# A decode kernel's list scheduler is given the fetch time of TensorE instructions, finer durations, and a new order of loads

## Chip, cores, metric

The kernel runs on one core of one Trainium2 chip. The metric is the device time of one execution, in microseconds (us), median over several runs. The profile's span (first to last instruction) is about 2 us shorter than the time of the same execution. Every comparison below is between runs of state "fast"; nothing slow was seen. One core means one die, so there is no second die to compare with.

Names used below: PE is TensorE and PEld its weight loads, DVE is VectorE, ACT is ScalarE, POOL is GpSimd, and SPq is the queue that sends out the loads. A load *lands* when all of its bytes are in place. An instruction page, or *page* for short, is a block of 256 instructions that PE fetches at once (the page *of a kernel* is the profiler's summary of it). "Planner" is the list scheduler.

## The reference, cut to what matters

A decode step of four transformer layers for batch B = 4 and one new token: attention layer, feed-forward layer, and the same two again. Both attention layers read the *same* caches.

```python
B, Sq, D = 4, 1, 512
Hq, Hkv, Sk, Dh = 32, 8, 8192, 128        # k_cache, v_cache: (B, Hkv, Sk, Dh) bf16, 67 MB each

def _A_ref(x, k_cache, v_cache, wq, wo):
    q = (x @ wq) ...                       # 4 query heads share one K/V head
    p = _softmax(einsum("bhqd,bhkd->bhqk", q, k) * Dh ** -0.5)
    return einsum("bhqk,bhkd->bhqd", p, v) ... @ wo
def _B_ref(x, w_gate, w_up, w_down):       # F = 1792
    return (_silu(x @ w_gate) * (x @ w_up)) @ w_down

x = x + _A_ref(_layernorm(x), k_cache, v_cache, wq, wo)
x = x + _B_ref(_layernorm(x), w_gate, w_up, w_down)
x = x + _A_ref(_layernorm(x), k_cache, v_cache, wq, wo)
x = x + _B_ref(_layernorm(x), w_gate, w_up, w_down)
```

The second attention layer of a batch element needs the first attention and feed-forward of *that element only*. So the kernel treats the four elements as four batches and interleaves layers: while batch 0 is between its layers, batch 1 is in its first.

## The kernel before

The kernel is a program that plans itself. While it is built, it makes a list of steps with an engine, an estimated duration and dependences; a list scheduler runs them through a small model and fixes the order of instructions of every engine. The order of *loads* is not decided by the scheduler: it is a string written by hand (or by a search). The loads go out in that order, each as soon as one of ten slots of 1 MB is free.

```python
class Plan:
    HOP = 0.2                    # us between a step and a dependent step on another engine
    LOAD_LEAD = 0.8
    LOAD_TAIL = 1.4
    ...
            at, s = best                         # the step that can start first
            s.start, s.end = at, at + s.us       # its duration is a constant
            free_at[s.eng] = s.end
    ...
    def emit(self):
        for s in sorted(self.steps + self.loads, key=lambda s: (s.start, s.prio[0])):
            s.fn()

ORDER = ("KKKqKVKKKoKKKgKKKKVKVVKKKgKuKKVoKVVVKKKVKKKVVKVVKVKKVVoVoVuddVKKKVKKKVKKVKKVKKKKKVKKKVKKVKVVKKVK"
         ... )                   # K, V: one 1 MB unit of a cache; q: wq; other letters: the next weight piece
KEPT = [5, 5, 5, 5]              # per batch: V units kept in their slot from layer 0 to layer 1, not loaded twice
NSLOT = 10
VCUT = [5, 5, 5, 8]
```

A K unit (4096 positions of one head) is transposed by DVE in place (2 instructions) and multiplied by PE (32 matmuls, so 64 instructions with their weight loads). After 16 K units of a batch, the softmax of that batch runs. A V unit is 32 matmuls on PE. After all V units of a first-layer batch comes its "chain": output projection, feed-forward, layer norm, q projection. The second-layer K units of that batch can be transposed before, but not multiplied; until the chain is done, they hold their slots.

```python
        NTAIL = [0, 3, 3, 3]
        vgroups = [(0, 0, g) for g in v_first(0)]
        rest = v_first(1)
        vgroups += [(0, 1, g) for g in rest[:G - NTAIL[1]]]
        for b in range(B):
            vgroups += [(1, b, g) for g in v_second(b)[:VCUT[b]]]
            if b + 1 < B:
                vgroups += [(0, b + 1, g) for g in v_first(b + 1)[G - NTAIL[b + 1]:]]
            vgroups += [(1, b, g) for g in v_second(b)[VCUT[b]:]]
            if b + 2 < B:
                vgroups += [(0, b + 2, g) for g in v_first(b + 2)[:G - NTAIL[b + 2]]]
```

This says which V unit each V of the string is: VCUT second-layer groups of batch b go ahead of the last NTAIL first-layer groups of batch b+1.

Of the kernel before, what the change touches and what calls it, by code (L numbers as in the profile page):

```python
# [5 lines left out]
ALU = mybir.AluOpType  # L6
# [5 lines left out]
class _Rec:  # L12
    __slots__ = ("w", "r")
# [89 lines left out]
class Step:  # L103
    __slots__ = ("eng", "us", "deps", "fn", "prio", "take", "free", "start", "end", "loads", "slot_of")

    def __init__(self, eng, us, fn, deps, prio, take=None, free=None):
        self.eng, self.us, self.fn, self.prio = eng, us, fn, prio
        self.deps = [d for d in deps if d is not None]
        self.take, self.free = take, free
        self.start = self.end = None  # L110
        self.slot_of = None


class Plan:

    HOP = 0.2
# [10 lines left out]
    def add(self, eng, us, fn, deps, prio, take=None, free=None):  # L127
        s = Step(eng, us, fn, deps, prio, take, free)
        self.steps.append(s)
        return s  # L130
# [7 lines left out]
    def run(self):  # L138
# [48 lines left out]

        self.slot = {}
        left = len(self.steps)
        pump(0.0)  # L190
        while left:
            best = None
            for e in engines:
                cand = None
                for t, s in todo[e]:
                    if s.take is not None:
                        b = min(bank_free.values()) if bank_free else None
                        if b is None:
                            continue
                        t = max(t, b)  # L200
                    at = max(t, free_at[e])
                    k = (at > free_at[e] + 1e-9, at if at > free_at[e] + 1e-9 else 0.0, s.prio[0])
                    if cand is None or k < cand[0]:
                        cand = (k, at, s)
                if cand is not None and (best is None or cand[1] < best[0]):
                    best = (cand[1], cand[2])
            nxt = None
            if li < len(self.loads) and (slots or self.loads[li].slot_of is None):
                nxt = max(sp_at, min(slots)[0] if self.loads[li].slot_of is not None else 0.0)
            if best is None and nxt is None:  # L210
                raise RuntimeError("the plan is stuck")
            if best is None or (nxt is not None and nxt <= best[0]):
                pump(nxt)
                continue
            at, s = best
            s.start, s.end = at, at + s.us
            free_at[s.eng] = s.end
            for i, (_, x) in enumerate(todo[s.eng]):
                if x is s:
                    todo[s.eng].pop(i)  # L220
                    break
            if s.take is not None:
                b = min(bank_free, key=lambda x: bank_free[x])
                del bank_free[b]
                held[s.take] = b
                self.bank[s.take] = b
            if s.free is not None:
                bank_free[held.pop(s.free)] = s.end + self.HOP
            if s.slot_of is not None:
                slots.append((s.end + self.HOP, self.slot[s.slot_of]))  # L230
            left -= 1
            finish(s)
# [4 lines left out]
    def emit(self):  # L237
        for s in sorted(self.steps + self.loads, key=lambda s: (s.start, s.prio[0])):
# [3 lines left out]
ORDER = ("KKKqKVKKKoKKKgKKKKVKVVKKKgKuKKVoKVVVKKKVKKKVVKVVKVKKVVoVoVuddVKKKVKKKVKKVKKVKKKKKVKKKVKKVKVVKKVK"  # L242
         "KKKKVKKKVVKVVVVVVVKVVVVVKVKVKKKKVKKVKKKVKKVKKVKKVKVKKVVKKVVKKKKKKKKVKVVVVVVVVVVVVKKKVKKKVVKKKKKK"
         "KKVKKVVVVVVVVVVVVVVVVVKVVVKKVKKKKKKKKKKKKKVVVVVVVVVVVVV")
KEPT = [5, 5, 5, 5]
NSLOT = 10
VCUT = [5, 5, 5, 8]


def bass_interleave_layers__gqa_block_cached__swiglu_ffn__decode_kernel(  # L250
# [33 lines left out]
    with ExitStack() as es:  # L284
# [107 lines left out]
        def col_sum(src, dst, key_in, key_out, deps, tag):  # L392
            def mm():
                bk = pbk(tag)
                op("pe", lambda e: e.matmul(ps[:, bk * BW:bk * BW + NQ * B], lhsT=onesm[:],  # L395
                                            rhs=src[:].rearrange("p n b -> p (n b)"), start=True, stop=True),
                   reads=["onesm", key_in], writes=[f"pb{bk}"])

            def rd():
                bk = pbk(tag)  # L400
                op("dve", lambda e: e.tensor_reduce(dst[:], ps[:, bk * BW:bk * BW + NQ * B].rearrange("p (n b) -> p b n", b=B),  # L401
                                                    AX.X, ALU.add), reads=[f"pb{bk}"], writes=[key_out])
            a = PL.add("pe", 0.6, mm, deps, CHAIN, take=tag)
            return PL.add("dve", 0.2, rd, [a], CHAIN, free=tag)
# [19 lines left out]
        def q_scale(dep):  # L424
            return PL.add("dve", 0.2, lambda: op("dve", lambda e: e.tensor_scalar(qscale[:], rstd[:], scale, None, op0=ALU.mult),
                                                 reads=["rstd"], writes=["qscale"]), [dep], CHAIN)

        def q_proj(heads, deps, tag):
            def mm():
                bk = pbk(tag)  # L430
                for h in heads:
                    for kt in range(KT):
                        op("pe", lambda e: e.matmul(ps[:, bk * BW + h * B:bk * BW + (h + 1) * B],  # L433
                                                    lhsT=wq_sb[:, kt, h * Dh:(h + 1) * Dh],
                                                    rhs=xnT[:, kt * B:(kt + 1) * B],
                                                    start=(kt == 0), stop=(kt == KT - 1)),
                           reads=["wq", "xnT"], writes=[f"pb{bk}"], sig=(kt == KT - 1 and h == heads[-1]))
            return PL.add("pe", 0.03 * KT * len(heads), mm, deps, CHAIN, take=tag)

        def q_spread(src, n, key, deps, tag):  # L440
# [9 lines left out]
            return PL.add("pe", 0.6, mm, deps, CHAIN, take=tag)  # L450
# [11 lines left out]
        def make_qpad1(b, dep, prior):  # L462
            k = kpos[(0, b)] % 2

            def fn():
                op("dve", lambda e: e.tensor_copy(q_diag(k, 0, G), qs1[:, :, :, :, b]),
                   reads=["qs1"], writes=[f"qpad{k}_0", f"qpad{k}_1"])
            st = PL.add("dve", 0.3, fn, [dep, prior], CHAIN)
            q_ready[(0, b)] = [st, st]
# [22 lines left out]
        def q_half(b, hf, mm_tag, deps, prior):  # L492
# [9 lines left out]
            s1 = PL.add("dve", 0.25, scl, deps, CHAIN, free=mm_tag)  # L502
# [8 lines left out]
            return PL.add("dve", 0.25, cp, [sp, prior], CHAIN, free=tag)  # L511
# [24 lines left out]
        def k_pair(u, ld, prio, prev):  # L536
# [3 lines left out]
            for h in range(2):  # L540
# [4 lines left out]
                tr.append(PL.add("dve", 1.22, t, [ld], prio))  # L545
# [18 lines left out]
            st = PL.add("pe", 1.95, qk, tr + [qd, prev] + (scores_free[0] or []), prio)  # L564
# [3 lines left out]
        def softmax(l, b, lastq, prio):  # L568
# [3 lines left out]
            for a in range(4):  # L572
# [10 lines left out]
                ex.append(PL.add("act", 0.9, x, [mx] + (p_free[q] or []), CHAIN))  # L583
# [5 lines left out]
            s = PL.add("dve", 0.2, g1, [mx], CHAIN)  # L589
# [5 lines left out]
            s = PL.add("pe", 0.3, g2, [s], CHAIN, take=n + "a")  # L595
# [12 lines left out]
            s = PL.add("pe", 0.5, g4, [s], CHAIN, take=n + "b")  # L608
# [4 lines left out]
            s = PL.add("dve", 0.2, g5, [s], CHAIN, free=n + "b")  # L613
# [11 lines left out]
            s = PL.add("dve", 1.3, g7, [al], CHAIN)  # L625
            for f in range(2):
# [13 lines left out]
                t_ = PL.add("pe", 1.1, tr, [s] if f == 0 else [s, t_], CHAIN, take=f"{n}t{f}")  # L640
                e_ = PL.add("act", 1.1, ev, [t_], CHAIN, free=f"{n}t{f}")
# [14 lines left out]
            s = PL.add("pe", 0.6, w2, [s], CHAIN, take=n + "l")  # L656
# [5 lines left out]
            inv_ready[(l, b)] = PL.add("dve", 0.4, w3, [s], CHAIN, free=n + "l")  # L662
# [4 lines left out]
        def oproj(l, g, deps, prio):  # L667
# [10 lines left out]
            return PL.add("pe", 0.55, fn, deps, prio)  # L678

        def v_group(l, b, g, lds, prios):  # L680
# [3 lines left out]
            for i, cp in enumerate(VCP):  # L684
# [15 lines left out]
                st = PL.add("pe", 1.0, pv, [prev, p_ready[(l, b)], lds.get(u)], prios[i], take=tag if i == 0 else None)  # L700
# [9 lines left out]
            n = PL.add("dve", 0.2, nm, [prev, inv_ready[(l, b)]], CHAIN, free=tag)  # L710
# [5 lines left out]
        def ffn_mm(w_sb, wname, deps, tag):  # L716
# [10 lines left out]
            return PL.add("pe", 1.75, fn, deps + [w_load[f"{wname}0"], w_load[f"{wname}1"]], CHAIN, take=tag)  # L727

        def ffn(dep, tag, dst=None, dkey="x"):
# [9 lines left out]
            s = PL.add("dve", 0.25, a1, [gate, root], CHAIN, free=tag + "g")  # L739
# [3 lines left out]
            s = PL.add("act", 0.3, a2, [s], CHAIN)  # L743
# [6 lines left out]
            s = PL.add("dve", 0.9, a3, [s], CHAIN)  # L750
# [6 lines left out]
            s = PL.add("dve", 0.45, a4, [s, up], CHAIN, free=tag + "u")  # L757
# [10 lines left out]
            s = PL.add("pe", 1.75, dn, [s, w_load["wd0"], w_load["wd1"]], CHAIN, take=tag + "d")  # L768
            return add_x(XT, "x", tag + "d", [s], dst, dkey)

        def add_x(base, key, tag, deps, dst=None, dkey="x"):
# [7 lines left out]
            return PL.add("dve", 0.2, fn, deps, CHAIN, free=tag)  # L779
# [34 lines left out]
        NTAIL = [0, 3, 3, 3]  # L814
# [78 lines left out]
        sx = PL.add("pe", 0.3, start_x, [boot], CHAIN, take="x")  # L893
        sx = PL.add("dve", 0.4, start_x2, [sx], CHAIN, free="x")
        cen, root = layer_norm(sx, "i")
        late = PL.add("dve", 2.0, setup_late, [cen], [-9.0])
# [56 lines left out]
        s = PL.add("pe", 0.6, fin1, [s], CHAIN, take="out")  # L953
# [42 lines left out]
```

## Time and profile before

| | before |
|---|---|
| time, median | 673.8 us when the prediction was made, 673.35 us in the run beside the changed kernel |
| span | 670.1 us |
| bytes on the load queue | 261.38 MB in 128 K, 108 V and 11 weight loads |
| last cache load lands | 654.2 us, 15.9 us before the end |
| what landings come late, summed | 28.4 us |

The last row is worked out from the trace: for each cache load, the time from the landing before it to its own, less the median of those times (2.485 us for 1.05 MB), summed over all cache loads.

First the page of the kernel before: busy time of the engines, the 40 slices of DMA share and GB/s, the queues, and the chain that ended last.

```profile
PE 459.3 (69%) x10672; PEld 272.4 (41%) x10672; DVE 377.7 (56%) x568; ACT 48.6 (7%) x114; POOL 2.7 (0%) x8
DMA  8999999999999999999899999999799999899890
GB/s 356 415 399 420 395 419 419 419 418 393 363 416 420 415 408 420 420 420 417 326 423 419 420 398 421 419 420 418 305 422 421 420 420 418 314 402 422 352 375 3
q1 hardware_dynamic: 41600, 261.38, 95.6%
q8 instruction: 83, 1.36, 0.8%
DMA 65%; PE 20%; DVE 9%; issue 4%; SPq 1%; ACT 1%; DVEq 0%
```

No engine is near full; the load queue is. So read the GB/s row first: 419 to 420 is a full slice, and each number well below is lost time (326, 305 and 314 in slices of 16.75 us, and the last three). The windows view gives the same by stretch. Its columns are the stretch, the busy time and number of instructions of PE, PEld, DVE, ACT and POOL, the granted clock, the DMA share and GB/s.

```profile
60.00:70.00 10.00, 4.26 (x71) 1.03 (x63) 3.14 (x3) 0.00 (x0) 0.00 (x0) 0.67 1.01 419
320.00:330.00 10.00, 7.68 (x227) 5.02 (x224) 5.54 (x9) 0.00 (x0) 0.00 (x0) 0.58 0.78 293
470.00:490.00 20.00, 14.03 (x357) 8.02 (x354) 14.90 (x19) 0.50 (x2) 0.00 (x0) 0.59 0.82 322
580.00:590.00 10.00, 9.05 (x268) 5.53 (x264) 5.93 (x12) 0.00 (x0) 0.00 (x0) 0.61 0.78 289
630.00:650.00 20.00, 13.39 (x418) 12.88 (x419) 1.70 (x10) 2.05 (x2) 0.00 (x0) 0.50 0.87 353
```

Why does the queue starve at 320? The timeline there (start, duration, instruction, and in brackets how long the engine sat idle before it and what ended that):

```profile
317.92 2.99 PE L433 MATMUL ps<-xnT,wq_sb 128*128 128x4 bf16 x107
322.86 0.70 PE L433 MATMUL ps<-xnT,wq_sb 128*128 128x4 bf16 x21 [1.95 <-issue]
324.65 0.28 PE L446 MATMUL ps<-qT,ident 128*32 128x16 bf16 x16
326.89 4.19 SPq L92 DMA_DIRECT2D pool<-in_A_k_cache_dram  x4
```

The q projection of a chain stops for 1.95 us in its middle, with no semaphore to wait for. "issue" means that. Only after the q projection and spreading (L446) can the waiting K units be multiplied, their slots come free, and four loads go out in a bunch at 326.9. That the stop is an instruction fetch is read from its pattern: PE has 21344 instructions (matmuls and weight loads), queue 8 moved 83 packets of 16 KB, one for 257 instructions, and in dense stretches those packets come 6.1 to 6.3 us apart. PE's waits on "issue" sum to 28.5 us, 13 of them over 1 us. Counting PE's instructions in the trace settles it: the three stops between 460 and 476 us come 256 instructions apart, and so do the last three, at 640, 646 and 652 us.

The end of the kernel, as the chain of waits tells it (start, duration, what):

```profile
639.68 0.51 PE ps L694 x19
640.19 2.00 issue
645.74 2.66 issue
651.95 2.66 issue
658.08 0.93 PE ps L694 x32
```

After the last softmax, PE has 16 V units and 8 pieces of output projection to do, 1280 instructions, and stops at three pages. It is done 5.6 us after the last load has landed.

### The profile page before, as it was taken

The numbers are of one execution on the slowest core, as the hardware profiler recorded it, in microseconds if no ns is written. First come the engines' busy times: TensorE is split into PE (matmuls) and PEld (weight loads), VectorE is DVE, ScalarE is ACT, GpSimd is POOL, SyncE is SP. The second block draws the span as 40 slices with busy tenths as digits, with TensorE's granted clock in tenths as the row PEclk, the third lists the DMA queues.
The fourth block names the chain that finished last, engine by engine and source line by source line (L and its number), as shares of the span: only waits on it lengthen the run. The fifth ranks groups of instructions, "written<-read, shape, count | busy, mean of one in ns | idle before, by whom it ended". The sixth has DMA issues, their size and how long they took to land.

```text
span 670.1 us, 22609 instructions
## 1 busy us (share of the span) xinstructions
PE 459.3 (69%) x10672; PEld 272.4 (41%) x10672; DVE 377.7 (56%) x568; ACT 48.6 (7%) x114; POOL 2.7 (0%) x8
## 2 busy tenths in 40 slices
PE   0555586676777687767777587777767765866566
PEld 0411153336532262357422253256422564722466
DVE  6467754544567867553476666742758502579302
ACT  1000110003000110021000110021000200000300
POOL 1000000000000000000000000000000000000000
PEclk9976565555555585555655585655656555577555
DMA  8999999999999999999899999999799999899890
GB/s 356 415 399 420 395 419 419 419 418 393 363 416 420 415 408 420 420 420 417 326 423 419 420 398 421 419 420 418 305 422 421 420 420 418 314 402 422 352 375 3
DMA packets 41693, 262.82 MB, mean 392 GB/s; under 512 B 3960, under 2 KB 9856, under 8 KB 10880
## 3 DMA queue, kind: packets, MB, share of 16 engines
q1 hardware_dynamic: 41600, 261.38, 95.6%
q8 instruction: 83, 1.36, 0.8%
q14 instruction: 10, 0.08, 0.0%
HBM read 261.36 MB, written 0.00 MB: 390 GB/s over the span
## 4 chain that ended last, share of the span: by engine, by line
DMA 65%; PE 20%; DVE 9%; issue 4%; SPq 1%; ACT 1%; DVEq 0%
DMA pool<-in_A_k_cache_dram 33%; DMA pool<-in_A_v_cache_dram 32%; PE ps L694 7%; PE ps L556 7%; DVE pool L544 6%; PE ps L433 2%; DVE negm L574 1%; SPq L92 1%; PE ps L632 1%; PE ps L672 1%; PE ps L721 1%; ACT pp L638 1%; PE ps L395 1%; PE ps L763 0%; DVE pp L623 0%
## 5 line engine op out<-in xcount | busy, mean ns | idle before, releaser
L544 DVE STREAM_TRANSPOSE pool<-pool 128x1024 uint32<-128x1024 uint32 x256 | 304.5, 1224 | 122.5 <-DMA pool<-in_A_k_cache_dram 117.0
L556 PE MATMUL ps<-pool,qpad 32*32 32x512 bf16 x4096 | 245.7, 571 | 77.4 <-DVE pool L544 72.1
L694 PE MATMUL ps<-pp,pool 128*128 128x4 bf16 x4096 | 125.1, 166 | 70.2 <-DMA pool<-in_A_v_cache_dram 51.3
L694 PEld LDWEIGHTS ps<-pp,pool 128*128 128x128 bf16 x4096 | 117.4, 104 | 105.9 <-DMA pool<-in_A_v_cache_dram 78.2
L556 PEld LDWEIGHTS ps<-pool,qpad 32*32 32x32 bf16 x4096 | 68.4, 113 | 207.2 <-DVE pool L544 133.7
L707 DVE TENSOR_TENSOR oT<-ps,invL 128x4 bf16<-128x4 f32 x64 | 10.3, 161 | 97.2 <-PE ps L694 97.2
L578 ACT ACTIVATE pp<-ps,negm 128x512 bf16<-128x512 f32 x32 | 21.5, 685 | 448.5 <-DVE negm L574 448.5
L433 PE MATMUL ps<-xnT,wq_sb 128*128 128x4 bf16 x640 | 18.4, 166 | 21.4 <-DMA wq_sb<-in_A_wq_dram 14.6
L672 PEld LDWEIGHTS ps<-oT,wo_sb 128*128 128x128 bf16 x640 | 20.6, 104 | 20.4 <-issue 11.9
L672 PE MATMUL ps<-oT,wo_sb 128*128 128x4 bf16 x640 | 23.3, 167 | 8.2 <-issue 2.7
L574 DVE TENSOR_REDUCE negm<-ps 128x1 f32<-128x512 f32 x32 | 19.8, 678 | 13.9 <-PE ps L556 13.9
L433 PEld LDWEIGHTS ps<-xnT,wq_sb 128*128 128x128 bf16 x640 | 18.5, 105 | 21.8 <-DMA wq_sb<-in_A_wq_dram 14.7
L638 ACT ACTIVATE pp<-ps 128x1024 bf16<-128x1024 bf16 x16 | 16.4, 1023 | 27.5 <-PE ps L632 27.4
L632 PE MATMUL ps<-ident,pp 128*128 128x128 bf16 x128 | 13.9, 278 | 5.1 <-ACT pp L638 3.3
L632 PEld LDWEIGHTS ps<-ident,pp 128*128 128x128 bf16 x128 | 10.6, 126 | 7.4 <-ACT pp L638 3.8
L419 ACT ACTIVATE lnv<-var,eps_sb 128x4 f32<-128x4 f32 x10 | 3.0, 297 | 112.5 <-DVE var L401 112.5
L763 PE MATMUL ps<-hT,wd_sb 128*128 128x4 bf16 x280 | 8.3, 166 | 3.4 <-issue 1.9
L721 PE MATMUL ps<-xnT,wu_sb 128*128 128x4 bf16 x280 | 8.2, 166 | 2.8 <-DVE oT L707 1.4
L623 DVE TENSOR_SCALAR pp<-pp,alpha 128x512 bf16<-128x512 bf16 x32 | 9.0, 343 | 1.8 <-ACT alpha L616 1.8
L763 PEld LDWEIGHTS ps<-hT,wd_sb 128*128 128x128 bf16 x280 | 7.9, 104 | 3.7 <-issue 3.0
L721 PEld LDWEIGHTS ps<-xnT,wu_sb 128*128 128x128 bf16 x280 | 7.9, 104 | 3.1 <-issue 1.6
L721 PEld LDWEIGHTS ps<-xnT,wg_sb 128*128 128x128 bf16 x280 | 8.8, 107 | 0.0
(65 smaller groups left out, 115.1 us busy)
## 6 DMA issues: line engine op xcount, KB each, us to landing
pool<-in_A_k_cache_dram SPq DMA_DIRECT2D x128, 1024.0 KB, 10.0
pool<-in_A_v_cache_dram SPq DMA_DIRECT2D x108, 1024.0 KB, 11.9
wq_sb<-in_A_wq_dram SPq DMA_DIRECT2D x1, 4096.0 KB, 18.4
wo_sb<-in_A_wo_dram SPq DMA_DIRECT2D x4, 1024.0 KB, 18.3
wg_sb<-in_B_w_gate_dram SPq DMA_DIRECT2D x2, 896.0 KB, 19.5
wu_sb<-in_B_w_up_dram SPq DMA_DIRECT2D x2, 896.0 KB, 19.7
wd_sb<-in_B_w_down_dram SPq DMA_DIRECT2D x2, 896.0 KB, 20.2
pp<-in_A_x_dram SPq DMA_DIRECT2D x1, 4.0 KB
```

The lines of the kernel that those rows point to most:

```text
L433: op("pe", lambda e: e.matmul(ps[:, bk * BW + h * B:bk * BW + (h + 1) * B], lhsT=wq_sb[:, kt, h * Dh:(h + 1) * Dh], rhs=xnT[:, kt * B:(kt ...
L544: op("dve", lambda e: e.transpose(v, v), reads=[key], writes=[key])
L556: op("pe", lambda e: e.matmul(ps[32 * c:32 * (c + 1), a * BW:(a + 1) * BW], lhsT=qpad[rows, qbuf, es_, g, :], rhs=ap[h][rows, :, es_ // 2, ...
L574: op("dve", lambda e: e.tensor_reduce(negm[:, q, a:a + 1], bank(a), AX.X, ALU.max, negate=True), reads=[f"pb{a}"], writes=[f"negm{q}_{a}"])
L578: op("act", lambda e: e.activation(pblk(q)[:, :, a, :], bank(a).rearrange("p (t j) -> p t j", j=32), ACTF.Exp, bias=negm[:, q, a:a + 1], s ...
L632: op("pe", lambda e: e.matmul(stg[:, t * P:(t + 1) * P], lhsT=pp[:, q, blk * P:(blk + 1) * P], rhs=ident[:], is_transpose=True, start=True ...
L638: op("act", lambda e: e.activation(pp[:, q, f * 1024:(f + 1) * 1024], bank_bf(bk)[:, :], ACTF.Copy), reads=[f"pb{bk}"], writes=pk(q))
L672: op("pe", lambda e: e.matmul(ps[:, OPJ * BW + nq * B:OPJ * BW + (nq + 1) * B], lhsT=wo_sb[:, h, nq * P:(nq + 1) * P], rhs=oT[:, l, h, :], ...
L694: op("pe", lambda e: e.matmul(ps[:, bk * BW:bk * BW + REP], lhsT=ap[:, t * Dh:(t + 1) * Dh], rhs=pp[:, q, col:col + REP], start=(i == 0 an ...
L707: op("dve", lambda e: e.tensor_tensor(oT[:, l, g * REP:(g + 1) * REP, b], ps[:, bk * BW:bk * BW + REP], invL[:, q, g * REP:(g + 1) * REP], ...
L721: op("pe", lambda e: e.matmul(ps[:, bk * BW + fo * B:bk * BW + (fo + 1) * B], lhsT=w_sb[:, kt, fo * P:(fo + 1) * P], rhs=xnT[:, kt * B:(kt ...
L763: op("pe", lambda e: e.matmul(ps[:, bk * BW + nq * B:bk * BW + (nq + 1) * B], lhsT=wd_sb[:, fo, nq * P:(nq + 1) * P], rhs=hT[:, fo * B:(fo ...
```

## The change

Its intent is to let the scheduler know that TensorE's instructions arrive in pages of 256, 6.2 us apart (what dense stretches showed), to correct the durations of the steps from a trace, and to search load order, kept units and group order again under that model. No instruction changes its work; the number of PE instructions is the same.

```diff
 class Plan:
-    HOP = 0.2
+    HOP = 0.06
+    PAGE = 6.2
+    PAGE_N = 256
...
+        def fetched(at, s):
+            nonlocal pe_n, page_at
+            if s.eng != "pe" or s.n == 0:
+                return at + s.us
+            first, pe_n = pe_n, pe_n + s.n
+            for k in range(first // self.PAGE_N + 1, pe_n // self.PAGE_N + 1):
+                there = at + s.us * (k * self.PAGE_N - first) / s.n
+                at += max(0.0, page_at + self.PAGE - there)
+                page_at = max(there, page_at + self.PAGE)
+            return at + s.us
...
-            s.start, s.end = at, at + s.us
+            s.start, s.end = at, fetched(at, s)
...
-ORDER = ("KKKqKVKKKoKKKgKKKKVKVVKKKgKuKKVoKVVVKKKVKKKVVKVVKVKKVVoVoVuddVKKKVKKKVKKVKKVKKKKKVKKKVKKVKVVKKVK"
+ORDER = ("VKdVKqKKKVKKKKKKKgKKKKVoVVKKKVKKKKVKKKVuKVVVVKVKuKKKVVVVgoodoVKVKVKKKKKKKKKKKKKKKVKKVVVVKVVVKKV"
...  (two more lines each; 13 V follow the last K before, 18 now)
-KEPT = [5, 5, 5, 5]
+KEPT = [5, 5, 4, 3]
-VCUT = [5, 5, 5, 8]
+VCUT = [1, 1, 0, 1]
+NTAIL = [0, 7, 5, 2]
...
-            st = PL.add("pe", 1.95, qk, tr + [qd, prev] + (scores_free[0] or []), prio)
+            st = PL.add("pe", 1.95, qk, tr + [qd, prev] + (scores_free[0] or []), prio, n=64)
...  (some 30 more steps get n, a duration changed by up to 1.2 us and mostly by under 0.2, or both)
-        NTAIL = [0, 3, 3, 3]
```

More of the change, by code (lines that the diff above doesn't have):

```diff
@@ L103, with __init__ @@
 class Step:
-    __slots__ = ("eng", "us", "deps", "fn", "prio", "take", "free", "start", "end", "loads", "slot_of")
-    def __init__(self, eng, us, fn, deps, prio, take=None, free=None):
+    __slots__ = ("eng", "us", "deps", "fn", "prio", "take", "free", "start", "end", "loads", "slot_of", "n")
+    def __init__(self, eng, us, fn, deps, prio, take=None, free=None, n=0):
+        self.n = n
         self.eng, self.us, self.fn, self.prio = eng, us, fn, prio
@@ L125, in __init__, with add @@
         self.bank = {}
-    def add(self, eng, us, fn, deps, prio, take=None, free=None):
-        s = Step(eng, us, fn, deps, prio, take, free)
+    def add(self, eng, us, fn, deps, prio, take=None, free=None, n=0):
+        s = Step(eng, us, fn, deps, prio, take, free, n)
         self.steps.append(s)
@@ L186, in pump @@
                 finish(s)
+        pe_n = 0
+        page_at = 0.0
+        def fetched(at, s):
[8 more added lines that the diff above has]
+            return at + s.us
         self.slot = {}
@@ L239, in emit @@
             s.fn()
-ORDER = ("KKKqKVKKKoKKKgKKKKVKVVKKKgKuKKVoKVVVKKKVKKKVVKVVKVKKVVoVoVuddVKKKVKKKVKKVKKVKKKKKVKKKVKKVKVVKKVK"
-         "KKKKVKKKVVKVVVVVVVKVVVVVKVKVKKKKVKKVKKKVKKVKKVKKVKVKKVVKKVVKKKKKKKKVKVVVVVVVVVVVVKKKVKKKVVKKKKKK"
-         "KKVKKVVVVVVVVVVVVVVVVVKVVVKKVKKKKKKKKKKKKKVVVVVVVVVVVVV")
-KEPT = [5, 5, 5, 5]
+ORDER = ("VKdVKqKKKVKKKKKKKgKKKKVoVVKKKVKKKKVKKKVuKVVVVKVKuKKKVVVVgoodoVKVKVKKKKKKKKKKKKKKKVKKVVVVKVVVKKV"
+         "KVKVKVKVKVKKKKVVKVVKKVKVKKVVKKVVVKKKKVVKKKKVVVVKKVKVKKKVKKVKVKKVKVVVKVKKVKVKKKVVKKKKKKVKKKKVKVK"
+         "VKKVVVVVVVVVVVVVVVVVVVVKVVKVKKKKKKKKKKKKKKVVVVVVVVVVVVVVVVVV")
+KEPT = [5, 5, 4, 3]
 NSLOT = 10
-VCUT = [5, 5, 5, 8]
+VCUT = [1, 1, 0, 1]
+NTAIL = [0, 7, 5, 2]
 def bass_interleave_layers__gqa_block_cached__swiglu_ffn__decode_kernel(
@@ L402, in rd @@
                                                     AX.X, ALU.add), reads=[f"pb{bk}"], writes=[key_out])
-            a = PL.add("pe", 0.6, mm, deps, CHAIN, take=tag)
-            return PL.add("dve", 0.2, rd, [a], CHAIN, free=tag)
+            a = PL.add("pe", 0.6, mm, deps, CHAIN, take=tag, n=8)
+            return PL.add("dve", 0.17, rd, [a], CHAIN, free=tag)
         def layer_norm(dep, tag):
@@ L424, in q_scale @@
         def q_scale(dep):
-            return PL.add("dve", 0.2, lambda: op("dve", lambda e: e.tensor_scalar(qscale[:], rstd[:], scale, None, op0=ALU.mult),
+            return PL.add("dve", 0.13, lambda: op("dve", lambda e: e.tensor_scalar(qscale[:], rstd[:], scale, None, op0=ALU.mult),
                                                  reads=["rstd"], writes=["qscale"]), [dep], CHAIN)
@@ L437, in mm @@
                            reads=["wq", "xnT"], writes=[f"pb{bk}"], sig=(kt == KT - 1 and h == heads[-1]))
-            return PL.add("pe", 0.03 * KT * len(heads), mm, deps, CHAIN, take=tag)
+            return PL.add("pe", 0.029 * KT * len(heads), mm, deps, CHAIN, take=tag, n=2 * KT * len(heads))
         def q_spread(src, n, key, deps, tag):
@@ L449, in mm @@
                            reads=["ident", key], writes=[f"pb{bk}"], sig=(es_ == NES - 1 and a == 3))
-            return PL.add("pe", 0.6, mm, deps, CHAIN, take=tag)
+            return PL.add("pe", 0.3, mm, deps, CHAIN, take=tag, n=32)
         def q_diag(k, g0, ng):
@@ L467, in fn @@
                    reads=["qs1"], writes=[f"qpad{k}_0", f"qpad{k}_1"])
-            st = PL.add("dve", 0.3, fn, [dep, prior], CHAIN)
+            st = PL.add("dve", 0.23, fn, [dep, prior], CHAIN)
             q_ready[(0, b)] = [st, st]
@@ L501, in scl @@
                    reads=[f"pb{bk}", "qscale"], writes=[f"qT2_{hf}"])
-            s1 = PL.add("dve", 0.25, scl, deps, CHAIN, free=mm_tag)
+            s1 = PL.add("dve", 0.21, scl, deps, CHAIN, free=mm_tag)
             tag = f"qs{b}_{hf}"
@@ L510, in cp @@
                    reads=[f"pb{bk}"], writes=[f"qpad{k}_{hf}"])
-            return PL.add("dve", 0.25, cp, [sp, prior], CHAIN, free=tag)
+            return PL.add("dve", 0.21, cp, [sp, prior], CHAIN, free=tag)
         home = {}
@@ L544, in t @@
                     op("dve", lambda e: e.transpose(v, v), reads=[key], writes=[key])
-                tr.append(PL.add("dve", 1.22, t, [ld], prio))
+                tr.append(PL.add("dve", 1.23, t, [ld], prio))
             qd = q_ready[(l, b)][2 * g // G]
@@ L582, in softmax @@
                 mx = PL.add("dve", 0.7, m, [lastq], CHAIN)
-                ex.append(PL.add("act", 0.9, x, [mx] + (p_free[q] or []), CHAIN))
+                ex.append(PL.add("act", 0.8, x, [mx] + (p_free[q] or []), CHAIN))
             scores_free[0] = ex
@@ L588, in g1 @@
                    reads=[f"negm{q}_{a}" for a in range(4)], writes=["gm"])
-            s = PL.add("dve", 0.2, g1, [mx], CHAIN)
+            s = PL.add("dve", 0.16, g1, [mx], CHAIN)
             def g2():
@@ L594, in g2 @@
                    reads=["gm", "identf"], writes=[f"pb{pbk(n + 'a')}"])
-            s = PL.add("pe", 0.3, g2, [s], CHAIN, take=n + "a")
+            s = PL.add("pe", 0.37, g2, [s], CHAIN, take=n + "a", n=2)
             def g3():
@@ L607, in g4 @@
                    reads=["rowm", "one1"], writes=[f"pb{bk}"])
-            s = PL.add("pe", 0.5, g4, [s], CHAIN, take=n + "b")
+            s = PL.add("pe", 0.58, g4, [s], CHAIN, take=n + "b", n=8)
             def g5():
@@ L612, in g5 @@
                 op("dve", lambda e: e.tensor_copy(gm[:], ps[:, bk * BW:bk * BW + 1]), reads=[f"pb{bk}"], writes=["gm"])
-            s = PL.add("dve", 0.2, g5, [s], CHAIN, free=n + "b")
+            s = PL.add("dve", 0.16, g5, [s], CHAIN, free=n + "b")
             def g6():
@@ L624, in g7 @@
                        reads=[f"pp{q}_{a}", f"alpha{q}"], writes=[f"pp{q}_{a}"])
-            s = PL.add("dve", 1.3, g7, [al], CHAIN)
+            s = PL.add("dve", 1.14, g7, [al], CHAIN)
             for f in range(2):
@@ L639, in ev @@
                        reads=[f"pb{bk}"], writes=pk(q))
-                t_ = PL.add("pe", 1.1, tr, [s] if f == 0 else [s, t_], CHAIN, take=f"{n}t{f}")
-                e_ = PL.add("act", 1.1, ev, [t_], CHAIN, free=f"{n}t{f}")
+                t_ = PL.add("pe", 1.0, tr, [s] if f == 0 else [s, t_], CHAIN, take=f"{n}t{f}", n=16)
+                e_ = PL.add("act", 1.03, ev, [t_], CHAIN, free=f"{n}t{f}")
             p_ready[(l, b)] = e_
@@ L655, in w2 @@
                    reads=["onesm", "selw"], writes=[f"pb{bk}"])
-            s = PL.add("pe", 0.6, w2, [s], CHAIN, take=n + "l")
+            s = PL.add("pe", 0.58, w2, [s], CHAIN, take=n + "l", n=8)
             def w3():
@@ L661, in w3 @@
                    reads=[f"pb{bk}"], writes=[f"invL{q}"])
-            inv_ready[(l, b)] = PL.add("dve", 0.4, w3, [s], CHAIN, free=n + "l")
+            inv_ready[(l, b)] = PL.add("dve", 0.35, w3, [s], CHAIN, free=n + "l")
         opj_n = [0]
@@ L677, in fn @@
                         opj_n[0] += 1
-            return PL.add("pe", 0.55, fn, deps, prio)
+            return PL.add("pe", 0.57, fn, deps, prio, n=32)
         def v_group(l, b, g, lds, prios):
@@ L699, in pv @@
                                reads=pk(q) + [key], writes=[f"pb{bk}"], sig=(h == 1 and t == NB - 1))
-                st = PL.add("pe", 1.0, pv, [prev, p_ready[(l, b)], lds.get(u)], prios[i], take=tag if i == 0 else None)
+                st = PL.add("pe", 1.0, pv, [prev, p_ready[(l, b)], lds.get(u)], prios[i], take=tag if i == 0 else None,
+                            n=64)
                 if not (l == 0 and (g, cp) in kept_of[b]):
@@ L709, in nm @@
                    reads=[f"pb{bk}", f"invL{q}"], writes=[f"oT{l}_{g}"])
-            n = PL.add("dve", 0.2, nm, [prev, inv_ready[(l, b)]], CHAIN, free=tag)
+            n = PL.add("dve", 0.17, nm, [prev, inv_ready[(l, b)]], CHAIN, free=tag)
             if l == 0 or b == B - 1:
@@ L726, in fn @@
                            sig=(kt == KT - 1 and fo == FO - 1))
-            return PL.add("pe", 1.75, fn, deps + [w_load[f"{wname}0"], w_load[f"{wname}1"]], CHAIN, take=tag)
+            return PL.add("pe", 1.64, fn, deps + [w_load[f"{wname}0"], w_load[f"{wname}1"]], CHAIN, take=tag, n=112)
         def ffn(dep, tag, dst=None, dkey="x"):
@@ L738, in a1 @@
                    reads=[f"pb{bk}", "rstd"], writes=["gs"])
-            s = PL.add("dve", 0.25, a1, [gate, root], CHAIN, free=tag + "g")
+            s = PL.add("dve", 0.22, a1, [gate, root], CHAIN, free=tag + "g")
             def a2():
                 op("act", lambda e: e.activation(eneg[:], gs[:], ACTF.Exp, scale=-1.0), reads=["gs"], writes=["eneg"])
-            s = PL.add("act", 0.3, a2, [s], CHAIN)
+            s = PL.add("act", 0.25, a2, [s], CHAIN)
             def a3():
@@ L749, in a3 @@
                 op("dve", lambda e: e.tensor_tensor(gs[:], gs[:], eneg[:], ALU.mult), reads=["gs", "eneg"], writes=["gs"])
-            s = PL.add("dve", 0.9, a3, [s], CHAIN)
+            s = PL.add("dve", 0.98, a3, [s], CHAIN)
             def a4():
@@ L756, in a4 @@
                 op("dve", lambda e: e.tensor_tensor(hT[:], gs[:], us[:], ALU.mult), reads=["gs", "us"], writes=["hT"])
-            s = PL.add("dve", 0.45, a4, [s, up], CHAIN, free=tag + "u")
+            s = PL.add("dve", 0.47, a4, [s, up], CHAIN, free=tag + "u")
             def dn():
@@ L767, in dn @@
                            reads=["hT", "wd0", "wd1"], writes=[f"pb{bk}"], sig=(fo == FO - 1 and nq == NQ - 1))
-            s = PL.add("pe", 1.75, dn, [s, w_load["wd0"], w_load["wd1"]], CHAIN, take=tag + "d")
+            s = PL.add("pe", 1.64, dn, [s, w_load["wd0"], w_load["wd1"]], CHAIN, take=tag + "d", n=112)
             return add_x(XT, "x", tag + "d", [s], dst, dkey)
@@ L778, in fn @@
                    reads=[key, f"pb{bk}"], writes=[dkey])
-            return PL.add("dve", 0.2, fn, deps, CHAIN, free=tag)
+            return PL.add("dve", 0.17, fn, deps, CHAIN, free=tag)
         def chain(b, deps, prior):
@@ L892, in bass_interleave_layers__gqa_block_cached__swiglu_ffn__decode_kernel @@
         boot = PL.add("dve", 2.2, lambda: None, [], CHAIN)
-        sx = PL.add("pe", 0.3, start_x, [boot], CHAIN, take="x")
+        sx = PL.add("pe", 0.3, start_x, [boot], CHAIN, take="x", n=8)
         sx = PL.add("dve", 0.4, start_x2, [sx], CHAIN, free="x")
         cen, root = layer_norm(sx, "i")
-        late = PL.add("dve", 2.0, setup_late, [cen], [-9.0])
+        late = PL.add("dve", 0.8, setup_late, [cen], [-9.0])
         qs1_ready = q_first(cen, PL.add("act", 0.01, lambda: None, [root, late], CHAIN))
@@ L952, in fin1 @@
                    reads=["xo", "ident"], writes=[f"pb{bk}"], sig=(nq == NQ - 1))
-        s = PL.add("pe", 0.6, fin1, [s], CHAIN, take="out")
+        s = PL.add("pe", 0.6, fin1, [s], CHAIN, take="out", n=8)
         def fin2():
```

## The prediction

> **What bounds it now.** The DMA queue. The page shows 69% busy for PE and 56% for DVE, but queue 1 moved 261.38 MB with a busy share of 95.6%, and the chain of waits is 65% DMA. In undisturbed stretches the windows view has 419 to 420 GB/s, one 1 MB load per 2.5 us. The last cache load lands at 654.2 us, 15.9 us before the end (670.1).
>
> The landings show where the queue starved. What each landing came later than 2.5 us after the one before sums to about 28 us. About 12 of that are single late landings in full stretches, which I expect to stay. About 16 are starvation: near 176 to 190 us (2.3), 330 (2.8), 483 to 488 (4.0), 584 to 593 (4.9), 640 to 644 (3.5). In the timeline, the middle three come while the K pairs of a second-layer batch sit in slots and wait for the chain (FFN, norm, q projection), which is itself stretched by PE gaps named "issue" (1.95 us at 320.9; 1.95, 2.26 and 2.27 us between 461 and 476). The last is the final softmax.
>
> **These gaps are the change's subject.** The Trainium skill, "Runtime: NRT & Kernel Launch", section "Instruction fetch mechanics", says that instructions come in 16 KiB blocks of 256, at a mostly hidden cost. The trace agrees with the size (83 packets, 1.36 MB on queue 8, for 21344 PE instructions), not with "hidden": in dense stretches the packets are 6.1 to 6.3 us apart, and PE idles 28 us on "issue" in the waits view.
>
> **What the change does.** Instructions and their work stay. The planner learns the page time (6.2 us per 256) and finer durations; the order of loads, groups and steps changes. Kept V units fall from 20 to 17: three more loads, 3.15 MB, at 2.5 us each +7.5 us, all on the critical path. NTAIL and VCUT move first-layer V groups ahead of second-layer ones: each chain starts earlier, with second-layer V work left to cover it. I expect this to recover 10 to 15 of the 16 us of starvation.
>
> **Tail.** Now 13 loads follow the last K load; after the final softmax PE has 16 units and 8 output projections, 1280 instructions, with three fetch gaps (2.00, 2.66, 2.66 us), and ends 5.6 us after the last landing. With 18 V loads after the last K, five of them of the batch before, the last landing should set the end, not the fetch: one unit (1.0), normalization, projection (0.6), last FFN and output (about 10.3), so about 12.5 us. Gain about 3 us.
>
> **Sum** (estimates from these numbers): +7.5 - 12.5 - 3 = -8 us. Time 673.8 - 8 = 666, range 660.5 to 672. Chances: faster by over 2% 0.08, within 2% 0.90, slower 0.02. Even with all starvation gone (-16), the sum is -12, short of 2% (13.5 us).
>
> **What would show it.** Right: queue 1 carries 264.5 MB in 111 V loads; full stretches still run at 419 to 420 GB/s; the dips in the DMA row are mostly filled; the last landing is near 650, the end 12 to 13 us later; PE's "issue" total hardly changes, but less of it is in the chain. Wrong: new starved stretches, as at the start, where a V, a weight piece and K stand before wq and the first QK waits about 2.5 us longer.
>
> **What would make it wrong.** The order was fitted to a model; where the chip drifts from it, the in-order queue meets slots not yet free and the 7.5 us are not paid back (about 674). If the late landings that I called fixed vanish too, it falls below 660.

## The result

| | before | changed |
|---|---|---|
| time, median | 673.35 us (672.62 to 673.85) | 664.5 us (663.65 to 665.55) |
| span | 670.1 | 662.4 |
| load queue | 261.38 MB, 108 V loads | 264.53 MB, 111 V loads |
| last cache load lands | 654.2 | 650.2 |
| from there to the end | 15.9 | 12.2 |
| late landings, summed | 28.4 | 16.7 |

The ratio of times is 0.9873 (95% interval 0.9857 to 0.9889). Ratios here and below are the mean time of one kernel's fast runs over that of the other's of the same rounds, so not quite the ratio of the medians.

The page of the changed kernel, same lines as above:

```profile
PE 459.8 (69%) x10672; PEld 276.0 (42%) x10672; DVE 375.7 (57%) x568; ACT 48.6 (7%) x114; POOL 2.7 (0%) x8
DMA  8999999999999999999999999999999999999991
GB/s 341 419 420 408 408 419 405 420 419 390 391 405 419 421 419 418 405 402 414 409 421 419 419 402 414 419 419 381 403 422 420 419 419 418 379 423 419 419 419 51
q1 hardware_dynamic: 42032, 264.53, 97.6%
q8 instruction: 83, 1.36, 0.8%
DMA 63%; PE 22%; DVE 11%; issue 2%; ACT 1%; SPq 1%
```

The work of the engines is what it was. The queue carries more and is fuller; the numbers near 300 are gone from the GB/s row, and the last slice is the only empty one. In the windows view, the same stretches as before:

```profile
60.00:70.00 10.00, 5.77 (x97) 1.68 (x97) 9.03 (x8) 0.00 (x0) 0.00 (x0) 0.66 1.01 410
320.00:330.00 10.00, 5.87 (x152) 2.97 (x136) 4.09 (x6) 0.42 (x1) 0.00 (x0) 0.67 1.01 413
470.00:490.00 20.00, 15.31 (x302) 5.93 (x303) 17.02 (x16) 1.02 (x1) 0.00 (x0) 0.67 0.99 406
580.00:590.00 10.00, 6.11 (x140) 1.82 (x128) 9.62 (x9) 0.00 (x0) 0.00 (x0) 0.95 1.01 425
630.00:650.00 20.00, 10.08 (x331) 9.33 (x327) 0.67 (x4) 0.00 (x0) 0.00 (x0) 0.50 0.91 374
```

(The last stretch reads low because the loads run out: the rate falls from 647 us on, and the last byte is in at 649.8.) The end, in the chain of waits:

```profile
626.45 2.06 issue
629.07 21.15 DMA pool<-in_A_v_cache_dram
650.22 0.05 issue
650.27 1.03 PE ps L712 x32
651.54 0.60 PE ps L690 x16
```

One page gap is left in the chain there, at 626. The load that goes out after it, at 629, stands in a queue that is full (it lands 21 us later), so from there on the chain is the load queue, and PE does one unit and one projection piece after the last landing.

The difference of the spans, 7.7 us, is therefore: three more loads, 3 x 2.485 = +7.5 us; late landings, 28.4 to 16.7 = -11.7 us; the end after the last landing, 15.9 to 12.2 = -3.7 us. The sum is -7.9 us. These are two single executions; the medians differ by 8.9 us, and in the repeat e7 the late landings sum to 17.9 us.

### The profile page after: what moved, and what is told of

The parts are those of the page before. It is cut to its first block, busy times and chain, and to the rows that moved or that the text cites. A ratio compares the mean times of both kernels' runs of the same rounds, so it can differ in the third digit from the quotient of the medians.

```text
span 662.4 us, 22618 instructions
## 1 busy us (share of the span) xinstructions
PE 459.8 (69%) x10672; PEld 276.0 (42%) x10672; DVE 375.7 (57%) x568; ACT 48.6 (7%) x114; POOL 2.7 (0%) x8
## 3 DMA queue, kind: packets, MB, share of 16 engines
q1 hardware_dynamic: 42032, 264.53, 97.6%
## 4 chain that ended last, share of the span: by engine, by line
DMA 63%; PE 22%; DVE 11%; issue 2%; ACT 1%; SPq 1%
DMA pool<-in_A_k_cache_dram 36%; DMA pool<-in_A_v_cache_dram 25%; PE ps L574 8%; DVE pool L562 8%; PE ps L712 7%; DMA wg_sb<-in_B_w_gate_dram 2%; PE ps L650 2%; PE ps L740 1%; PE ps L451 1%; DVE negm L592 1%; SPq L92 1%; ACT pp L656 1%; PE ps L690 1%; DVE pp L641 1%; PE ps L782 1%
## 5 line engine op out<-in xcount | busy, mean ns | idle before, releaser
L574 PE MATMUL ps<-pool,qpad 32*32 32x512 bf16 x4096 | 241.1, 563 | 65.7 <-DVE pool L562 60.6
L712 PE MATMUL ps<-pp,pool 128*128 128x4 bf16 x4096 | 126.6, 166 | 64.0 <-DMA pool<-in_A_v_cache_dram 46.8
L592 DVE TENSOR_REDUCE negm<-ps 128x1 f32<-128x512 f32 x32 | 19.8, 677 | 9.9 <-PE ps L574 9.9
L650 PE MATMUL ps<-ident,pp 128*128 128x128 bf16 x128 | 16.5, 310 | 6.1 <-ACT pp L656 3.7
L656 ACT ACTIVATE pp<-ps 128x1024 bf16<-128x1024 bf16 x16 | 16.4, 1023 | 29.6 <-PE ps L650 29.6
L650 PEld LDWEIGHTS ps<-ident,pp 128*128 128x128 bf16 x128 | 12.3, 141 | 9.5 <-ACT pp L656 4.4
L740 PE MATMUL ps<-xnT,wg_sb 128*128 128x4 bf16 x280 | 8.2, 166 | 1.3 <-DMA wg_sb<-in_B_w_gate_dram 1.3
L413 PE MATMUL ps<-XT,onesm 128*128 128x16 f32 x20 | 6.0, 382 | 3.4 <-DVE XT L795 2.9
```

The source lines that it names most:

```text
L574: op("pe", lambda e: e.matmul(ps[32 * c:32 * (c + 1), a * BW:(a + 1) * BW], lhsT=qpad[rows, qbuf, es_, g, :], rhs=ap[h][rows, :, es_ // 2, ...
L592: op("dve", lambda e: e.tensor_reduce(negm[:, q, a:a + 1], bank(a), AX.X, ALU.max, negate=True), reads=[f"pb{a}"], writes=[f"negm{q}_{a}"])
L650: op("pe", lambda e: e.matmul(stg[:, t * P:(t + 1) * P], lhsT=pp[:, q, blk * P:(blk + 1) * P], rhs=ident[:], is_transpose=True, start=True ...
L656: op("act", lambda e: e.activation(pp[:, q, f * 1024:(f + 1) * 1024], bank_bf(bk)[:, :], ACTF.Copy), reads=[f"pb{bk}"], writes=pk(q))
L712: op("pe", lambda e: e.matmul(ps[:, bk * BW:bk * BW + REP], lhsT=ap[:, t * Dh:(t + 1) * Dh], rhs=pp[:, q, col:col + REP], start=(i == 0 an ...
L740: op("pe", lambda e: e.matmul(ps[:, bk * BW + fo * B:bk * BW + (fo + 1) * B], lhsT=w_sb[:, kt, fo * P:(fo + 1) * P], rhs=xnT[:, kt * B:(kt ...
```

## The experiments

**Theory A:** the load order, with the group order that belongs to it, lets the queue run full; the scheduler's new numbers only served to find it. **Rival B:** the scheduler's better order of engine steps removed the stalls, whatever the loads' order. **Rival C,** for the end: it is bound by instruction fetch and no order of loads helps.

All kernels gave the right result. The table collects them.

| run | what it is | time, median | ratio to before | last landing | to the end | late landings |
|---|---|---|---|---|---|---|
| e1 | new scheduler, old order | 678.9 | 1.0081 | 661.6 | 15.6 | 35.7 |
| e2 | old scheduler, new order | 669.9 | 0.9947 | 656.3 | 12.2 | 22.2 |
| e3 | changed, page time 0 | 666.6 | 0.9901 | 653.3 | 12.2 | 19.8 |
| e4 | before, tail alone | 668.0 | 0.9952 | 651.6 | 14.0 | 26.0 |
| e10 | before, groups alone | 674.1 | 1.0018 | 657.5 | 16.0 | 31.5 |
| e5 | changed, 4 more loads | 673.6 | 1.0041 | 659.6 | 12.2 | 16.4 |
| e6 | changed, idle matmuls | 665.9 | 0.9908 | 650.3 | 12.2 | 16.5 |
| e7 | changed, again | 664.75 | 0.9892 | 651.5 | 12.2 | 17.9 |
| e8 | 18 kept, searched anew | 663.3 | 0.9876 | 649.1 | 12.3 | 17.0 |
| e9 | 19 kept, searched anew | 674.1 | 1.0038 | 660.4 | 12.2 | 31.7 |

### The scheduler alone and the order alone

```diff
 # e1: the changed kernel with
-KEPT = [5, 5, 4, 3]      VCUT = [1, 1, 0, 1]      NTAIL = [0, 7, 5, 2]      ORDER = (new)
+KEPT = [5, 5, 5, 5]      VCUT = [5, 5, 5, 8]      NTAIL = [0, 3, 3, 3]      ORDER = (that of before)
 # e2: the kernel before with the four new values
 # e3: the changed kernel with
-    PAGE = 6.2
+    PAGE = 0.0
```

> The changed planner (page time, finer durations, HOP 0.06) with the load order, kept units (20), VCUT and NTAIL of before. Theory A (the load order and the group order removed the starvation; the planner's numbers only found it): the starved stretches stay, queue 1 moves 261.4 MB, the last landing stays near 654 us, time 670 to 676 us. Rival B (the planner's new order of engine steps removed the stalls, whatever the load order): the dips fill, the last landing is near 643 to 646 and the time 659 to 664 us.

> The planner of before (no page time, coarse durations, HOP 0.2) with the new load order, 17 kept units, new VCUT and NTAIL. Theory A: nearly all of the gain is there, 664 to 668 us, last landing 650 to 653. Rival B: the three extra loads are paid for and the dips stay, 675 to 682 us.

> The changed kernel with the planner's page time set to 0; all else as in the changed kernel. Theory A: same as the changed kernel within 2 us (663 to 667): the loads' order is fixed by hand, and each engine's own order hardly turns on the page time. Rival B: the page time is what orders the steps well, so 3 us or more are lost (over 667).

e1 was *slower* than before, by 0.8% (interval 0.5 to 1.1%), outside what either theory expected. Its GB/s row still has the holes, and deeper:

```profile
GB/s 356 414 401 419 397 417 418 420 417 394 318 409 419 418 415 420 419 419 411 274 421 420 420 403 421 419 420 417 278 422 418 420 420 417 292 369 421 370 372 6
```

The timeline of e1 shows in one place what happened:

```profile
322.92 1.25 DVE L562 STREAM_TRANSPOSE pool<-pool 128x1024 uint32<-128x1024 uint32 x1 [5.06 <-DMA pool<-in_A_k_cache_dram]
324.33 0.29 PE L464 MATMUL ps<-qT,ident 128*32 128x16 bf16 x16 [3.09 <-DVE qT L517]
```

The plan has the transpose of a K unit ahead of the chain's small scaling step (qT) on DVE. The unit had not landed; DVE sat 5.06 us on the load, took up qT only after it, at 324.1 us, and the chain's PE step waited 3.09 us for that. A finer model is no safer on an order that was not made with it. Rival B falls.

e2 is faster than before (ratio 0.9947, interval 0.9915 to 0.998), but by some 3 us, not 9; the expected 664 to 668 us was missed. It has the short end (12.2 us), and its landings lose 22.2 instead of 16.7 us. Its largest loss is a landing 3.8 us late at 465 us. The timeline of e2 ahead of it:

```profile
449.29 9.31 SPq L92 DMA_DIRECT2D pool<-in_A_v_cache_dram  x2
449.56 3.65 PE L433 MATMUL ps<-xnT,wq_sb 128*128 128x4 bf16 x128
457.17 1.01 PE L556 MATMUL ps<-pool,qpad 32*32 32x512 bf16 x9 [2.33 <-issue]
```

The old scheduler ran both halves of the q projection in one piece, 256 instructions in 3.65 us, and PE then stood 2.33 us at a page in the middle of a K unit's product. No slot came free between the two loads that went out at 449.3 and 458.3, so the queue ran dry. In the changed kernel the same chain, at nearly the same time, has the halves apart, with other units between:

```profile
445.02 1.86 PE L451 MATMUL ps<-xnT,wq_sb 128*128 128x4 bf16 x64 [1.10 <-DVE var L419]
449.50 1.86 PE L451 MATMUL ps<-xnT,wq_sb 128*128 128x4 bf16 x64
452.14 0.25 PE L464 MATMUL ps<-qT,ident 128*32 128x16 bf16 x10 [0.61 <-issue]
453.42 6.92 SPq L92 DMA_DIRECT2D pool<-in_A_k_cache_dram  x4
```

The page costs 0.61 us there, and the next load goes out at 453.4. So Theory A holds in part only. The new order brought a part of the gain by itself, the new scheduler with the old order none: of the 1.27% that the time fell, about 0.5% is there with the new order under the old scheduler, and the rest comes only with both. e3 puts a size on the page time within that: 666.6 against 664.5 and 664.75 us for the changed kernel, about 2 us, with intervals that overlap (0.9872 to 0.9929 against 0.9857 to 0.9889); it lies at the upper end of what Theory A expected. How the scheduler's share splits between the page time and the durations with HOP is not shown. By the medians, durations and HOP (e2 to e3) give 3.3 us and the page time (e3 to changed) 2.1; by the late landings it is 2.4 and 3.1.

A rival stands untested: no new search was made under the *old* scheduler. So the record does not show that the finer model was needed to find a better order; searching again might have done as well.

### Parts of the order, without any extra load

```diff
 # e4: the kernel before with
-          "KKVKKVVVVVVVVVVVVVVVVVKVVVKKVKKKKKKKKKKKKKVVVVVVVVVVVVV")
+          "KKVKKVVVVVVVVVVVVVVVVVKVKKKKKKKKKKKKKKKVVVVVVVVVVVVVVVV")
-VCUT = [5, 5, 5, 8]
+VCUT = [5, 5, 0, 8]
 # e10: the kernel before with
-VCUT = [5, 5, 5, 8]           NTAIL = [0, 3, 3, 3]
+VCUT = [1, 1, 0, 1]           NTAIL = [0, 7, 5, 2]
```

> The kernel before (its planner, its 20 kept units, so no extra load) with one part of the change: VCUT of the third batch 0 instead of 5 (its second-layer V groups all come after the last first-layer ones), and three of the V loads in front of the last K loads moved behind them, so 16 loads instead of 13 follow the last K. Theory A (the tail and the last chain were one part of the loss): the starved stretches near 584 to 593 (4.9 us) and 640 to 644 (3.5 us) shrink and the end comes 12 to 13 us after the last landing instead of 15.9; 662 to 667 us. Rival C (the tail is bound by PE's instruction fetch, whatever the order of loads): the end is only moved by what the dip at 584 gives back, 668 us or more.

> The kernel before with the new VCUT and NTAIL alone: its planner, its order of load kinds and its 20 kept units stay, so no extra load; only which V group each V letter means changes, so each first-layer batch ends earlier and second-layer V groups come later. If the earlier chains alone fill the dips, as the prediction's step on NTAIL and VCUT reads, the dips near 330, 483 to 488 and 584 to 593 us fade and the time is 662 to 668 us. If an order of K and V made for the old groups starves elsewhere, no gain, 671 us or more: group order and load order then have to be changed together.

e4 came out between its two expectations, at 668.0 us (ratio 0.9952). The last dip, which the prediction had at 640 to 644 us, is gone from its GB/s row, and the end takes 14.0 us after the last landing instead of 15.9. The dip ahead of it, near 580, stayed (278 in the row below). So the two edits of e4, not told apart, are worth 3.5 us by the medians of the same chip (671.5 to 668.0), 4.5 by the spans (670.1 to 665.6). Rival C falls in one half: the order of loads does help. Its other half holds in e4, whose chain still has all three page stops. They are as long as before; the V products after the last softmax only start earlier (629.3 instead of 634.4 us). The end is still 1.8 us longer than in the changed kernel, which has 18 loads there and one stop left in its chain. Here are e4's GB/s row and the stops from its chain of waits:

```profile
GB/s 354 417 398 420 394 418 419 419 418 393 376 412 419 419 408 420 420 419 417 313 418 423 419 411 413 419 420 419 313 420 420 419 420 404 278 419 420 418 419 30
635.14 1.94 issue
640.64 2.66 issue
646.85 2.66 issue
```

e10 gained nothing (ratio 1.0018, interval 0.9991 to 1.0045). Late landings grew to 31.5 us, with dips now near 318 us (one landing 3.4 us late) and at 576 to 592:

```profile
GB/s 356 414 399 420 396 416 420 419 417 395 349 420 419 416 413 419 417 407 288 422 402 424 420 393 418 420 420 408 364 419 420 420 419 357 302 418 422 360 376 4
```

This is what was expected if the K and V pattern was fitted to the old groups: which V group a letter stands for cannot be moved without moving the letters.

### The price of one load

```diff
 # e5: the changed kernel with 4 V added to ORDER, three of them in its last third
-KEPT = [5, 5, 4, 3]
+KEPT = [5, 5, 0, 3]
```

> The changed kernel with 13 instead of 17 kept units (the third batch keeps none), so four V units more are loaded, spread over the order. If a load costs its full time on the queue, as the prediction has it (2.5 us each, plus a little of the late landings), the time rises by 9.5 to 11.5 us over the changed kernel, to 674 to 677 us. If fewer held slots give something back, by less than 8 us.

The median rose by 9.1 us (664.5 to 673.6), the last landing by 9.4 us, 2.3 us per load. By the two ratios to the kernel before it is 1.0041/0.9873, or 11 us. The median is just under the expected 674 to 677. So each load costs about its full time, as the prediction counted, and the three kept units that the change gave up cost about 7 us. In this kernel, which keeps the fewest units in slots, the late landings are 16.4 us, as in the changed kernel (16.7). No run came below it, so it is called the floor here; that the changed kernel has hardly any starvation left is inferred from it.

### What the floor is

In the changed kernel single loads land 0.9 to 1.4 us late at 35.2, 107.2, 178.2, 241.6 and 295.3 us, though many loads are queued and the rate is full. Counting the packets of queue 8 in the trace, these are the landings after PE instruction pages 1, 9, 17, 25 and 33: one in eight. The kernel before has them after the same pages, at 29.7, 110.5, 176.1, 244.8 and 305.9 us. (The 1.3 to 1.6 us in the expectation below are too high for the last two, 0.9 and 1.1.)

```diff
 # e6: the changed kernel with, after the 32 matmuls of each K unit
+                if l == 0 and b < 2:
+                    for n in range(16):
+                        op("pe", lambda e: e.matmul(ps[:, OPJ * BW + 64:OPJ * BW + 68], lhsT=ident[:], rhs=ident[:, 0:4],
+                                                    start=(u == kseq[0] and n == 0), stop=False, skip_group_check=True),
+                           reads=["ident"], sig=False)
```

> The changed kernel with 16 extra small matmuls after each of the first 32 K units (first two batches): 1024 more PE instructions, 4 more instruction pages, between about 30 and 150 us; nothing reads what they write, the order of everything else is the same. It asks what the single late landings are (1.3 to 1.6 us late after pages 1, 9, 17, 25 and 33 in the changed kernel, at 35.2, 107.2, 178.2, 241.6 and 295.3 us). If every eighth PE instruction page makes a landing late, they come after the same page counts, so at earlier loads: page 9 before 90 us, page 17 before 150 us. If they come from the loads themselves (every 26 or so loads), they stay at about 107 and 178 us. The time should stay within 3 us of the changed kernel.

With the extra instructions, page 9 came earlier and so did the late landing: 94.9 instead of 107.2 us; page 17's at 148.8 instead of 178.2. The first is 5 us later than the expected limit, the second within it. They follow the pages, not the loads. The span is the same (662.5). So instruction pages are not only possible stops of PE: after every eighth, in this first half of the run, the data queue lost up to 1.4 us. Later the pattern is less regular in the changed kernel, as a dip or a smaller lateness breaks the count; in e6 it is again every eighth from page 41 to page 81. For 83 pages, that is ten times 0.9 to 1.4, an estimate of 9 to 14 us, the larger part of the floor of 16.4.

The trace shows a part of why it is not every page. Each load ends with 16 packets of 4 bytes, one at the end of each of 16 streams that carry it. In the changed kernel the 16 of one load come within 0.25 us of each other before page 1. After page 1 (31.6 us) one of them comes 1.4 us behind the rest, after page 2 two do, after page 3 three. So a page sets back one stream. A load has landed when the last of the 16 is in, so page 1 made a landing late, and pages 2 and 3, which hit other streams, did not. Every eighth would follow if the pages went round eight streams; that was not traced through the run and is not shown.

### A version with more kept units

As each load costs its time, fewer loads should pay if the queue does not starve. Orders for 18 and 19 kept units were searched with the kernel's own scheduler, its load time set to 2.55 us, which is what the landings show on average with the late ones.

```diff
 # e8, e9: the changed kernel with
-KEPT = [5, 5, 4, 3]      VCUT = [1, 1, 0, 1]      NTAIL = [0, 7, 5, 2]      load 2.5
+KEPT = [5, 5, 5, 3]      VCUT = [5, 0, 1, 1]      NTAIL = [0, 0, 4, 6]      load 2.55      # e8, and a new ORDER
+KEPT = [5, 6, 4, 4]      VCUT = [1, 1, 3, 5]      NTAIL = [0, 1, 5, 0]      load 2.55      # e9, and a new ORDER
```

> The changed kernel itself, word for word, as the yardstick on the chip of the next two runs: 663 to 667 us, ratio to the kernel before 0.986 to 0.990.

> The changed kernel with 18 kept units (5, 5, 5, 3) instead of 17, an order of loads, VCUT and NTAIL searched anew, and the planner's time of one load at 2.55 instead of 2.5 us (what the landings show on average with the late ones). If a load's price of 2.5 us is the whole story and nothing starves, 2 to 3 us less than the changed kernel; if the tighter slots starve the queue, equal or slower.

> The same with 19 kept units (5, 6, 4, 4). The load's price gives 5 us less; the planner already sees about 3 us of starvation in it, so 1 to 3 us less than the changed kernel is expected, with more excess of the landings than in the run with 18.

e7 came out as expected. e8 had the lowest median of all, 663.3 against 664.75 us for the changed kernel on the same chip, 1.5 us less (2 to 3 were expected). The ratios to the kernel before are 0.9876 (0.9854 to 0.9897) and 0.9892 (0.9872 to 0.9913); they overlap, so a gain over the changed kernel is likely but not shown. e9 missed its expectation by over 10 us: its late landings rose to 31.7 us, where the scheduler's model had seen about 3 us of starvation. That two more kept units hold slots for longer is the likely reason; it was not tested. Of the newly searched orders, those with 17 and 18 kept units kept the queue full and the one with 19 did not; that no order with 19 can is not shown.

## Why the prediction was right

- **The sum.** Predicted +7.5 - 12.5 - 3 = -8 us; the trace has +7.5 - 11.7 - 3.7 = -7.9. Predicted time 666, measured 664.5. Each term held within 1 us of these single executions (with e7's trace the second is -10.5). e5 supports the first by itself.
- **The end.** "the last landing should set the end, not the fetch ... about 12.5 us": 12.2 us, and the chain of waits there is the V load. "the last landing is near 650": 650.2.
- **Signs named.** 264.53 MB, 111 V loads, filled dips, full stretches at 419 to 420 GB/s: all there. No new starvation showed at the start, though the first QK began at 33.5 instead of 27.7 us, 5.8 us later and not 2.5.
- **Wrong in part: "PE's 'issue' total hardly changes".** It fell from 28.5 to 23.2 us. Its share of the chain fell from 3.6% to 2.2%, as expected.
- **Right as a fact, not enough as a cause: "NTAIL and VCUT move first-layer V groups ahead ... each chain starts earlier".** In the changed kernel the feed-forward of the last three chains starts 31, 28 and 19 us earlier (at 272.7, 429.0 and 549.9 instead of 304.2, 457.1 and 568.5 us). In e10 the two values alone brought it forward by only 7 to 10 us, and the dips stayed. The recovery of 11.7 us came only with the new K/V order, the groups and the scheduler together; the parts do not add (e1 +0.8%, e2 -0.5%, all -1.3%).
- **Right without knowing why: "About 12 of that are single late landings ..., which I expect to stay".** They stayed; e6 shows the two that it tested to follow the instruction pages. One loss that the prediction counted as starvation, at 176 us, is of this kind too (page 17) and stayed, at 178.2.
- **The bound.** "Even with all starvation gone (-16), the sum is -12, short of 2%" is what kept the chance of over 2% low. Measured: 1.27%, with a floor of 16.4 us of late landings still there.

The Trainium skill, "Runtime: NRT & Kernel Launch", section "Instruction fetch mechanics", gave the reading of the gaps: pages of 16 KiB, 256 instructions. This trace agrees on the size, 83 packets of 16 KB for 21344 PE instructions, and differs on the cost.

## What to carry to other kernels

When a queue is the bound, sum how much later than the steady pace each landing comes: that number is the most that any reordering can win ahead of the last landing, and it is to be set against the bytes that the new order adds. Here the order of loads, the groups it stands for and the order of steps on in-order engines acted as one object; half of a tuned set can be worse than the old whole, so search again when the scheduler's model changes. Before tuning on, look for what the floor is made of: here, by the estimate above, the larger part is instruction fetch, so fewer PE instructions, and not a better order, would be the next thing to try (this was not tried).

## What the Trainium skill lacked or had wrong

- "Runtime: NRT & Kernel Launch", "Instruction fetch mechanics", says that the cost of crossing a page is mostly hidden and that dispatch is slower than the fill. Here PE's waits that name nothing sum to 28.5 us in the kernel before, up to 2.8 us at a time, and dense stretches got one page in 6.1 to 6.3 us.
- The same section has no number for a page's time, or what it depends on. In the kernel before, pages followed each other after 3.5 to 3.9 us where the load queue was running out (294, 323 and 4 GB/s after the pages at 473.2, 579.5 and 655.8 us), and after 6.1 us where it was full (419 to 420 GB/s after those at 461.0 and 467.1).
- No page says that instruction pages hold up data loads: a landing came 0.8 to 1.6 us late after pages 1, 9, 17, 25 and 33, in both kernels, and in e6 those of pages 9 and 17 moved with the pages. Each of the first three pages set one of a load's 16 streams back by about 1.4 us.
- "DMA: Bandwidth & Descriptors", "Where 436 GB/s comes from", says that for HBM to SBUF the HBM side of about 358 GB/s binds. Without a condition, that does not hold here: full stretches ran at 419 to 420 GB/s, HBM reads by the one core in use. The page's own table of single-core measurements, in its section "Measured", has 425 GB/s for 16 MB, which agrees.
